# Inverting triangles of 16 on VectorE and joining them to 32 on TensorE, in a chunked linear-attention kernel with an MLP behind it

## The chip, the cores and the metric

The kernel runs on one core of one Trainium2 chip. The metric is the device time of one execution in microseconds; lower is better. The time of the kernel before is the median of three runs.

## The reference

For each of 4 x 8 = 32 heads, with 768 time steps and a head dimension of 40, a 40 x 40 state is carried from step to step:

```
y[t]  = r[t] @ state
Sa    = state @ a[t]
state = state * w[t] - outer(Sa, b[t]) + outer(v[t], k[t])
```

The outputs of all heads are laid side by side to rows of 320 numbers, 3072 rows in all, and go through an MLP: `h = x @ w_in` (320 to 2048), `g = h * tanh(softplus(h))`, `out = g @ w_out` (2048 to 320). All inputs and outputs are float32.

## The kernel before

**Chunks and heads.** The 768 steps are cut into 12 chunks of 64. Within a chunk the recurrence is written with matrices. For each chunk and head a 64 x 64 triangle of products between `a` and `b` has to be inverted; what is left of the recurrence is a few small products and a state that goes from chunk to chunk. The 32 heads are held as two halves `be` = 0 and 1, each with 16 heads.

**Units.** The program is written as units with short names, a letter, a chunk and a half or group:

- `l` loads `wa` (decays and `a`) and `bk` (`b` and `k`) of a chunk and a half by SyncE's queue. There are two buffers of each kind (`NWA = 2`), so that the load of a half waits until the half two places earlier is used up.
- `p` (scan, L287 to L302) forms running products of the decays on VectorE: a reduction L287, two scans L289 and L296, products L294 and L300.
- `g` (gram, L317) makes the products of `a` with `b` and `k` on TensorE. ScalarE copies them to `GP` (L318, L321), VectorE masks the other part to `HA` (L322).
- `k` (natural, L333, L339, L346) transposes `bk` and `a` on TensorE.
- `i` (inverse, L353 to L365) works on a pair of chunks, that is on 64 triangles of 64 x 64, each seen as two 32 x 32 triangles on its diagonal and one 32 x 32 square, the corner, below them. VectorE masks the 128 diagonal triangles, transposes them so that each lies along a partition, and inverts all at once by forward substitution: 30 steps, each a product L360 into `tmp` and a sum L362 into `XL`. Three transposes in all (L355, L364, L365) lay them in and out. A step needs the result of the step ahead of it.
- `b` (blocks, L390) and `m` (corner, L374 and L382) build the 64 x 64 inverse in `T64`: TensorE multiplies the square from the right and from the left by the two inverted triangles, ScalarE copies between (L378) and behind (L385). There are two tiles `T64`.
- `t` (merge, L401) multiplies `HA` by `T64`; `KT` is copied by ScalarE (L403).
- `V`, `A`, `B`, `T`, `D`, `C` are the steps of the state for a chunk and a group of heads: `A` L431, `T` L439, `D` L447, `B` L459 with VectorE's mask L462, `C` L481 and L488 with VectorE's L491 and L495.
- `v`, `u`, `q`, `o` are loads and stores by GpSimd's queue; `w` and `W` load the MLP's weights and split them in two parts on ScalarE and VectorE; `x` and `X` load the attention's result for the MLP; `h` (L653), `H` (L660, L661), `y` (L674 to L676) and `z` (L680) are the MLP.

**Order.** Two tables of names fix the order by hand. `SEQ` is the order in which the units are written down; `PLAN` gives for each engine how many instructions of which unit follow on one another. Each engine works its list strictly in that order. VectorE's list mixes the steps of an inverse with scans of later chunks, instruction by instruction. TensorE's list holds the MLP's first products (`h`) between the steps of the last two chunks, and nothing but the MLP after them.

**Buffers.** `g`, `k`, `t`, `m` and `h` write to one PSUM pool (`pa`) of two tiles, 4 KB per partition each. The inverse's `GP` has two tiles, `TT` and `XL` one.

A program's float32 product stands twice among the trace's matmuls: a row x64 in the trace is 32 products of the program. A product of fp32r (the MLP's) and a transpose stand once.

Of the kernel before, what the change touches and what calls it, by code (L numbers as in the profile page):

```python
# [2 lines left out]

# [5 lines left out]
F32 = mybir.dt.float32  # L9
# [10 lines left out]
NWA = 2  # L20
NKT = 4
NXL = 1
NTT = 1
NYEV = 1
# [198 lines left out]
def attention(ctx, tc, I, yD, pD, nch, M, U):  # L223
# [22 lines left out]
    with ln('z'):  # L246
# [5 lines left out]
        for t in T64[:NT64]:  # L252
            G.memset(t, 0.0)
# [12 lines left out]
    def ld(c, be):  # L266
# [8 lines left out]
        if (c, be) == (0, 0):  # L275
            LQ.dma_start(out=cst, in_=I['cst'])
# [519 lines left out]
```

## Time and profile before

| what | value |
|---|---|
| three runs | 750.04, 752.26, 752.87 us |
| median | 752.26 us |
| the profiled execution | 749.9 us, its span 748.1 us |
| TensorE's mean granted clock in it | 0.958 of full |
| busy share of the span: TensorE, VectorE, ScalarE, GpSimd | 87%, 61%, 48%, 14% |
| share of the chain that ended last: TensorE, VectorE, ScalarE, DMA | 68%, 15%, 6%, 5% |
| merges of the first pair of chunks begin, of the last pair | 96.1 us, 367.7 us |
| first product of the MLP begins | 392.6 us |

The profile is read in two stages. Up to some 390 us the attention runs, with many small products on TensorE and a full VectorE; behind that the MLP, with TensorE full. The span is shorter than the run's time by 1.8 us, which lie around it. The granted clock is that of TensorE alone: 1.00 is full speed. The profile's records of it begin at 101 us; what lies ahead of them is shown as full.

### The profile page before, as it was taken

To read this page: it belongs to the slowest core of one execution; us is meant where nothing else is said; L and a number is where in the kernel's file an instruction comes from. 1 tells how busy PE (TensorE), PEld (TensorE's weight loads), DVE (VectorE), ACT (ScalarE), POOL (GpSimd) and SP (SyncE) were. 2 spreads that over 40 slices of the span, in tenths; PEclk is the share of its full clock that TensorE was granted. 3 is DMA by queue.
4 is the path that set the end of the run, shared out by engine and by line. 5 is a ranking of instruction groups with operands and counts; after the bars stand their busy time and mean duration, and the time that the engine had idled before them with its cause. 6 is when DMAs were issued, how large, how long until landed. Compare 5 with 4: busy or idle time off the path is not lost.

```text
span 748.1 us, 22984 instructions
## 1 busy us (share of the span) xinstructions
PE 652.8 (87%) x10184; PEld 583.2 (78%) x10184; DVE 455.8 (61%) x901; ACT 359.2 (48%) x571; POOL 104.9 (14%) x181
## 2 busy tenths in 40 slices
PE   2645799789798879888889999999999999999997
PEld 1443688688687778777778889998988989989997
DVE  7689999799899999999267768521222122111100
ACT  2222556655575846687566655532333323323311
POOL 7211013223223313212120000000000000000000
PEclk9999999779879989979899999999999999999999
DMA  7433215334524624334266543130101100100001
GB/s 211 111 90 88 82 32 152 92 83 124 135 68 102 160 64 121 80 96 129 85 196 179 156 151 106 44 115 1 36 29 57 35 1 1 36 1 1 35 1 37
DMA packets 31348, 62.12 MB, mean 83 GB/s; under 512 B 6800, under 2 KB 19216, under 8 KB 31248
## 3 DMA queue, kind: packets, MB, share of 16 engines
q1 hardware_dynamic: 22800, 40.91, 18.3%
q0 software_dynamic: 8448, 19.73, 10.7%
q8 instruction: 80, 1.31, 0.8%
q14 instruction: 20, 0.16, 0.1%
HBM read 48.77 MB, written 11.80 MB: 81 GB/s over the span
## 4 chain that ended last, share of the span: by engine, by line
PE 68%; DVE 15%; ACT 6%; issue 6%; DMA 5%; SPq 0%; DVEq 0%; ACTq 0%
PE pa L653 24%; PE pu L676 4%; PE pu L674 4%; PE pu L675 4%; PE pq L676 4%; PE pq L675 4%; PE pq L674 4%; DMA wa<-in_wa 3%; PE pa L317 3%; PE pq L459 3%; DVE XL L362 3%; PE pq L481 3%; DVE tmp L360 3%; PE pa L401 2%; PE pa L333 2%
## 5 line engine op out<-in xcount | busy, mean ns | idle before, releaser
L661 DVE TENSOR_TENSOR gl<-g,gh 128x1024 fp32r<-128x1024 f32 x48 | 58.7, 1224 | 186.2 <-ACT gh L660 186.0
L653 PE MATMUL pa<-xh,w_ih 128*128 128x512 f32 x288 | 113.1, 393 | 0.0
L654 ACT ACTIVATE g<-pa 128x1024 f32<-128x1024 f32 x48 | 49.3, 1027 | 99.3 <-PE pa L653 86.1
L653 PE MATMUL pa<-xh,w_il 128*128 128x512 f32 x288 | 96.7, 390 | 0.0
L660 ACT CAST gh<-g 128x1024 fp32r<-128x1024 f32 x48 | 50.2, 1048 | 61.9 <-PE pq L675 58.7
L653 PE MATMUL pa<-xl,w_ih 128*128 128x512 f32 x192 | 74.8, 390 | 0.0
L317 PE MATMUL pa<-bk,wa 40*64 40x128 f32 x768 | 36.5, 337 | 35.5 <-DMA bk<-in_bk 14.2
L653 PEld LDWEIGHTS pa<-xh,w_il 128*128 128x128 f32 x288 | 54.1, 188 | 11.4
L653 PEld LDWEIGHTS pa<-xh,w_ih 128*128 128x128 f32 x288 | 54.1, 188 | 10.6
L362 DVE TENSOR_TENSOR XL<-XL,tmp 128x30 f32<-128x30 f32 (+9 forms) x180 | 59.0, 328 | 2.6
L360 DVE TENSOR_TENSOR tmp<-XL 128x30 f32<-128x30 f32 (+9 forms) x180 | 58.6, 326 | 2.8
L317 PEld LDWEIGHTS pa<-bk,wa 40*64 40x64 f32 x768 | 29.0, 169 | 39.8 <-DVE bk L300 25.9
L676 PE MATMUL pq<-w_oh,gl 128*128 128x320 f32 x192 | 59.3, 309 | 0.0
L676 PE MATMUL pu<-w_oh,gl 128*128 128x320 f32 x192 | 59.3, 309 | 0.0
L675 PE MATMUL pq<-w_ol,gh 128*128 128x320 f32 x192 | 59.3, 309 | 0.0
L674 PE MATMUL pq<-w_oh,gh 128*128 128x320 f32 x192 | 59.3, 309 | 0.0
L674 PE MATMUL pu<-w_oh,gh 128*128 128x320 f32 x192 | 59.2, 309 | 0.0
L675 PE MATMUL pu<-w_ol,gh 128*128 128x320 f32 x192 | 59.2, 308 | 0.0
L302 POOL DMA_DIRECT2D pD<-P x48 | 35.2, 738 | 127.7 <-DVE w L292 52.9
L481 PE MATMUL pq<-UVQ,bkn 128*64 128x104 f32 (+1 forms) x768 | 40.9, 262 | 11.7 <-DVE UVQ L462 7.1
L481 PEld LDWEIGHTS pq<-UVQ,bkn 128*64 128x64 f32 x768 | 36.4, 143 | 15.7 <-issue 9.1
L653 PEld LDWEIGHTS pa<-xl,w_ih 128*128 128x128 f32 x192 | 36.1, 188 | 6.2
(93 smaller groups left out, 1338.0 us busy)
## 6 DMA issues: line engine op xcount, KB each, us to landing
wa<-in_wa SPq DMA_DIRECT2D x48, 162.5 KB
bk<-in_bk SPq DMA_DIRECT2D x48, 160.0 KB
cv_d<-in_wi SPq DMA_DIRECT2D x12, 512.0 KB
cv_d<-in_wo SPq DMA_DIRECT2D x16, 320.0 KB
VS<-in_vN POOLq DMA_DIRECT2D x24, 160.0 KB, 4.1
bdr<-in_rD POOLq DMA_DIRECT2D x24, 160.0 KB, 3.6
pD<-P POOLq DMA_DIRECT2D x48, 80.0 KB, 3.0
UVT<-in_vD POOLq DMA_DIRECT2D x24, 160.0 KB, 3.9
```

The source lines that it names most:

```text
L302: PQ.dma_start(out=pD[c, be, :, al].rearrange("e (s t) -> e s t", t=64), in_=P3[al * 64:al * 64 + 40, :, 0:64])
L317: PE.matmul(pt[o, al, s // 2], a[q, s], bk[q, s], start=(s < 2), stop=True, skip_group_check=True)
L360: V.tensor_tensor(out=tv, in0=X[:, i + 1:32, i:i + 1].broadcast_to([128, 31 - i, i]), in1=X[:, i:i + 1, 0:i].broadcast_to([128, 31 - i, i] ...
L362: V.tensor_tensor(out=X[:, i + 1:32, 0:i], in0=X[:, i + 1:32, 0:i], in1=tv, op=ALU.add)
L481: PE.matmul(py[be * 64:be * 64 + 64, al, s, 0:n], BKN[c, be][:, u * 40:u * 40 + 64], UVQ[be][:, u, 0:n], start=(s == 0), stop=(c == 0), sk ...
L653: PE.matmul(pt[:, j], w, x, start=(n == 0), stop=(n == 7), skip_group_check=True)
L654: A.activation(g, pt, AF.Mish)
L660: A.copy(gh, g)
L661: V.tensor_tensor(out=gl, in0=g, in1=gh.bitcast(F32), op=ALU.subtract)
L674: PE.matmul(po[i][k], gh[:, j, t], oh, start=(f == 0), stop=False, skip_group_check=True)
L675: PE.matmul(po[i][k], gh[:, j, t], ol, start=False, stop=False, skip_group_check=True)
L676: PE.matmul(po[i][k], gl[:, j, t], oh, start=False, stop=(f == 15), skip_group_check=True)
```

## The change

**The inverse.** VectorE inverts triangles of 16 instead of 32. `inverse` transposes `GP` into `DD` (L367), masks the two 16 x 16 triangles on the diagonal of each 32 x 32 triangle into `XD` (L368), and does 14 steps of a product and a sum (L374, L376) on both triangles of a partition at once; two transposes (L378, L379) lay the result in `TT` and, transposed, in `DD`. The mask of 1024 numbers (L353) goes.

**The join.** A new unit `j` for each pair of chunks makes 32 x 32 inverses out of the 16 x 16 ones on TensorE, in four diagonal tiles of the array (partitions 0 to 31, 32 to 63, 64 to 95, 96 to 127, each with the same columns). It has one product with an identity in fp32r (L384), 128 small float32 products (L388), a copy by ScalarE to `Z` (L389), 128 products (L393), 64 products (L397), and five copies by ScalarE (L398, L401). All of them use one PSUM tile `pa`.

**The corner.** It is one unit for a pair of chunks instead of two, with the same 128 products (L413, L416), one copy between instead of two for each half, and four behind.

**Exchanged halves.** For the heads of `be` = 1 the two halves of a chunk in `a` are exchanged, so that their triangles come to lie on the other partitions of their tile; the copies of `gram` and `merge`, a mask and a scan's product (now two instructions) follow that.

**Loads and order.** Four buffers for `wa` and `bk` instead of two. `SEQ` and `PLAN` are new throughout.

```diff
-NWA = 2
+NWA = 4
+NDD = 1
 SEQ = '''
-    l0.0 l0.1 p0.0 p0.1 v0 g0.0 k0.0 u0 q0 g0.1 l1.0 k0.1 l1.1 p1.0 p1.1 g1.0 k1.0 g1.1 k1.1 l2.0 i0 l2.1 p2.0 p2.1 g2.0
+    l0.0 p0.0 l1.0 l1.1 l0.1 p0.1 p1.0 g0.0 k0.0 g0.1 p1.1 l2.0 p2.0 k0.1 g1.0 g1.1 i0 k1.1 l2.1 l3.1 g2.0 v0 u0 k1.0 l3.0
...
-    wa[..., 528:] = a.transpose(4, 2, 1, 6, 3, 0, 5).reshape(nch, 2, 2, 40, 512)
+    at = a.transpose(4, 2, 1, 6, 3, 0, 5).reshape(nch, 2, 2, 40, 8, 2, 32).copy()
+    at[:, 1] = at[:, 1, ..., ::-1, :].copy()
+    wa[..., 528:] = at.reshape(nch, 2, 2, 40, 512)
...
-        V.tensor_tensor(out=gp[:, :, 1], in0=gp[:, :, 1], in1=maskG.unsqueeze(1).broadcast_to([128, 32, 32]), op=ALU.mult)
-        X = iw.tile([128, 32, 32], F32, name="XL", bufs=NXL)
-        V.transpose(X.rearrange("p t j -> p j t"), gp[:, :, 1].rearrange("p u j -> p j u"))
-        V.memset(X.rearrange("p t j -> p (t j)")[:, 0:1024:33], 1.0)
-        for i in range(1, 31):
-            tmp = iw.tile([128, 240], F32, name="tmp", bufs=NTMP)
...
+        V.transpose(X0[:, 0:1024].rearrange("p (j t) -> p j t", t=32), gp[:, :, 1].rearrange("p u j -> p j u"))
+        V.tensor_tensor(out=d, in0=d0, in1=mask16.unsqueeze(1).broadcast_to([128, 2, 16, 16]), op=ALU.mult)
+        V.memset(XD[:, 0:1024:33], 1.0)
+        for i in range(1, 15):
+            m = 15 - i
+            tmp = iw.tile([128, 112], F32, name="tmp", bufs=NTMP)
+            tv = tmp[:, 0:2 * i * m].rearrange("p (b j t) -> p b j t", j=i, t=m)
+            V.tensor_tensor(out=tv, in0=d[:, :, i:i + 1, i + 1:16].broadcast_to([128, 2, i, m]),
+                            in1=d[:, :, 0:i, i:i + 1].broadcast_to([128, 2, i, m]), op=ALU.mult)
+            V.tensor_tensor(out=d[:, :, 0:i, i + 1:16], in0=d[:, :, 0:i, i + 1:16], in1=tv, op=ALU.add)
...
+    def join(n):
+        gp, tt, dd = GP[n], TT[n], DD[n]
+        pt = ps_a.tile([128, 2, 512], F32, name="pa").rearrange("p x (u t) -> p x u t", t=16)
+        PE.matmul(pt[:, 0], identR, eyeR.unsqueeze(1).broadcast_to([128, 32, 16]), start=True, stop=True, skip_group_check=True)
+        for u in range(32):
+            for k in range(4):
+                q = slice(k * 32, k * 32 + 32)
+                PE.matmul(pt[k * 32:k * 32 + 16, 0, u], gp[q, u, 1, 0:16], tt[q, u, 16:32], start=False, stop=True, skip_group_check=True)
+        A.copy(Z[:, :, 16:32], pt[:, 0])
+        for u in range(32):
+            for k in range(4):
+                q = slice(k * 32, k * 32 + 32)
+                PE.matmul(pt[q, 1, u], dd[q, u], Z[q, u, 16:32], start=(u == 0), stop=True, skip_group_check=True)
+        for c2, x in product(range(2), range(8)):
+            for h, be in product(range(2), range(2)):
+                q, u = slice(h * 64 + be * 32, h * 64 + be * 32 + 32), c2 * 16 + be * 8 + x
+                PE.matmul(pt[q, 0, u], Z[q, u], dd[q, u, 0:16], start=(c2 + x == 0), stop=True, skip_group_check=True)
+        A.copy(tt[:, :, 16:32], pt[:, 1])
+        for h, be in product(range(2), range(2)):
+            q = slice(h * 64 + be * 32, h * 64 + be * 32 + 32)
+            A.copy(pick(dd[q], be)[:, :, :, 0:16], pick(pt[q, 0], be))
...
-        A.copy(kt, pk)
+        k4, p4 = (x.rearrange("p h a s (y t) -> p (h a s) y t", y=2) for x in (kt, pk))
+        A.copy(k4[:, :, ::-1] if be else k4, p4)
```

**What moves, at three places.** The first is TensorE's list at the fifth pair of chunks, from the gram of chunk 11 to the merge of chunks 8 and 9. Before (L317 is `g`, L333, L339 and L346 are `k`, L447 is `D`, L374 and L382 are the corner, L401 is the merge):

```order
L317 MATMUL pa<-bk_93,wa_91 64x128 x16
L333 MATMUL pa<-cst,bk_93 128x128 x8
L447 MATMUL pu<-cst,ST_112 128x128 x4
L339 MATMUL pa<-cst,wa_91 128x128 x4
L374 MATMUL pa<-TT,GP 32x32 x32
L346 MATMUL pa<-w_4675,cst 64x16 x2
L346 MATMUL pa<-w_4868,cst 64x16 x2
L374 MATMUL pa<-TT,GP 32x32 x32
L382 MATMUL pa<-X_5208,GP 32x32 x32
L447 MATMUL pu<-cst,ST_113 128x128 x4
L382 MATMUL pa<-X_5278,GP 32x32 x32
L401 MATMUL pa<-T_95,HA 64x64
```

The same place now (L384, L388, L393 and L397 are the join, L413 and L416 the corner, L482 is `D`, L344 and L350 are `k`, L435 is the merge):

```order
L482 MATMUL pu<-cst,ST_125 128x128 x4
L384 MATMUL pa<-eyeR,identR 128x512
L388 MATMUL pa<-TT,GP 16x16 x128
L482 MATMUL pu<-cst,ST_126 128x128 x4
L393 MATMUL pa<-Z,DD 32x16 x128
L397 MATMUL pa<-DD,Z 32x16 x64
L413 MATMUL pa<-TT,GP 32x32 x64
L416 MATMUL pa<-X_6376,DD 32x32 x64
L344 MATMUL pa<-cst,bk_100 128x128 x8
L350 MATMUL pa<-cst,wa_96 128x128 x4
L435 MATMUL pa<-T_103,HA 64x64
```

The 128 products of the corner now have 321 of the join ahead of them, with one short step of the state (L482) between, and stand closed up instead of among other units.

The second place is VectorE's list where the first inverse begins. Before (L355 to L362 belong to the inverse, L287, L288, L289, L292 and L294 to a scan, L322 to a gram):

```order
L287 TENSOR_REDUCE w_474<-wa_90 128x8
L355 STREAM_TRANSPOSE XL<-GP 128x32x32
L288 RECIPROCAL d_94<-w_474 128x8
L356 MEMSET XL 128x32
L360 TENSOR_TENSOR tmp<-XL 128x30
L322 TENSOR_TENSOR HA<-pa,cst 128x8x64
L362 TENSOR_TENSOR XL<-XL,tmp 128x30
L289 SCALAR_TENSOR_TENSOR P<-wa_90,d_94 128x520
L360 TENSOR_TENSOR tmp<-XL 128x58
L292 COPY w_474<-P 128x8
```

Now (L307 ends a scan, L367 to L376 belong to the inverse):

```order
L307 SCALAR_TENSOR_TENSOR E<-wa_94,d_102 128x519
L367 STREAM_TRANSPOSE DD<-GP 128x1024
L368 TENSOR_TENSOR XD<-DD,cst 128x2x16x16
L369 MEMSET XD 128x32
L374 TENSOR_TENSOR tmp<-XD 128x28
L376 TENSOR_TENSOR XD<-XD,tmp 128x2x14
L374 TENSOR_TENSOR tmp<-XD 128x52
L376 TENSOR_TENSOR XD<-XD,tmp 128x2x2x13
L374 TENSOR_TENSOR tmp<-XD 128x72
```

The scan of chunk 2 that was mixed with the first steps of the inverse stands ahead of it now, and the first half of the steps follow on one another.

The third place is TensorE's list behind the grams of the first pair, now (L328 is `g`, L344, L350 and L357 are `k`, the other names are as above):

```order
L384 MATMUL pa<-eyeR,identR 128x512
L328 MATMUL pa<-bk_99,wa_95 64x128 x16
L388 MATMUL pa<-TT,GP 16x16 x64
L344 MATMUL pa<-cst,bk_99 128x128 x8
L388 MATMUL pa<-TT,GP 16x16 x64
L350 MATMUL pa<-cst,wa_95 128x128 x4
L393 MATMUL pa<-Z,DD 32x16 x64
L357 MATMUL pa<-w_275,cst 64x16 x2
L357 MATMUL pa<-w_834,cst 64x16 x2
L393 MATMUL pa<-Z,DD 32x16 x64
L328 MATMUL pa<-bk_100,wa_96 64x128 x16
L397 MATMUL pa<-DD,Z 32x16 x64
```

Here grams and transposes of chunks 2 and 3 stand between the join's parts; before, all of them stood ahead of the first corner.

More of the change, by code (lines that the diff above doesn't have):

```diff
@@ L2 @@
 from functools import partial
+from itertools import product
 import numpy as np
@@ L144 @@
+        h5.7 H5.7 z5.0 z5.1 z5.2 z5.3
     ''',
     'Pool': '''
[L146 to L149 removed]
@@ L213, in layouts @@
     p = np.arange(128)
-    cst = np.zeros((128, 288), np.float32)
+    cst = np.zeros((128, 608), np.float32)
     cst[:, :128] = np.eye(128)
@@ L293, in scan @@
         a3 = a.rearrange("p (s t) -> p s t", t=64)
-        V.scalar_tensor_tensor(out=a3, in0=a3, scalar=-1.0, in1=P3[:, :, 0:64], op0=ALU.mult, op1=ALU.mult)
+        for o, i in ((slice(0, 32), slice(32, 64)), (slice(32, 64), slice(0, 32))) if be else ((slice(0, 64), slice(0, 64)),):
+            V.scalar_tensor_tensor(out=a3[:, :, o], in0=a3[:, :, o], scalar=-1.0, in1=P3[:, :, i], op0=ALU.mult, op1=ALU.mult)
         V.reciprocal(d1[:, 64:584:65], w2[:, 1])
@@ L370, in corner, with pick @@
+    def pick(x, be):
+        return x.rearrange("p (c b s) t -> p c b s t", b=2, s=8)[:, :, be]
+    def corner(n):
+        gp, tt, dd = GP[n], TT[n], DD[n]
         pt = ps_a.tile([128, 2, 512], F32, name="pa").rearrange("p x (u t) -> p x u t", t=32)
-        for j in range(16):
-            for k in range(2):
-                q, o = slice(k * 64 + 32, k * 64 + 64), slice(k * 64, k * 64 + 32)
-                PE.matmul(pt[o, 0, j], gp[q, h * 16 + j, 0], tt[q, h * 16 + j], start=(j == 0), stop=True, skip_group_check=True)
@@ L375, in corner @@
         X = iw.tile([128, 16, 32], F32, name="X2", bufs=NX2)
-        for k in range(2):
-            q = slice(k * 64, k * 64 + 32)
-            A.copy(X[q], pt[q, 0])
-        for j in range(16):
-            for k in range(2):
-                q = slice(k * 64, k * 64 + 32)
-                PE.matmul(pt[q, 1, j], gp[q, h * 16 + j, 1], X[q, j], start=(j == 0), stop=True, skip_group_check=True)
-        for k in range(2):
-            q = slice(k * 64, k * 64 + 32)
-            A.copy(T64[n % 2][q, us, 32:64], pt[q, 1])
+        its = [(c2 * 8 + x, c2 * 16 + be * 8 + x, h * 64 + 32 - be * 32, h * 64 + be * 32)
+               for c2, x, h, be in product(range(2), range(8), range(2), range(2))]
@@ new lines, in corner @@
+        for j, u, q, o in its:
+            PE.matmul(pt[o:o + 32, 0, j], gp[q:q + 32, u, 0], tt[q:q + 32, u], start=(j == 0), stop=True, skip_group_check=True)
+        A.copy(X, pt[:, 0])
+        for j, u, q, o in its:
+            PE.matmul(pt[o:o + 32, 1, j], dd[o:o + 32, u], X[o:o + 32, j], start=(j == 0), stop=True, skip_group_check=True)
+        for h, be in product(range(2), range(2)):
+            q = slice(h * 64 + be * 32, h * 64 + be * 32 + 32)
+            A.copy(pick(T64[n % 2][q], be)[:, :, :, 32 - be * 32:64 - be * 32], pt[q, 1].rearrange("p (c s) t -> p c s t", c=2))
@@ L512, in attention @@
         U['i%d' % n] = partial(inverse, n)
+        U['j%d' % n] = partial(join, n)
         U['b%d' % n] = partial(blocks, n)
-        for h in range(2):
-            U['m%d.%d' % (n, h)] = partial(corner, n, h)
+        U['m%d' % n] = partial(corner, n)
     U['/p'] = pctx.close
```

240 lines of the change are left out of this document (121 added, 119 removed).

## The prediction

> **What bounds the kernel now.** I read the page first, then windows of the trace, then single stretches of its timeline. The page says which engine is full where:
>
> ```profile
> span 748.1 us, 22984 instructions
> PE   2645799789798879888889999999999999999997
> DVE  7689999799899999999267768521222122111100
> PEclk9999999779879989979899999999999999999999
> ```
>
> A digit is a slice of 18.7 us. VectorE is full from the second slice to the nineteenth. TensorE is full only from the twenty-second, where the MLP runs alone; ahead of that it has gaps, and its granted clock falls again and again. So there are two stages: an attention of some 390 us that VectorE seems to bound, and an MLP that TensorE bounds and that the change doesn't touch.
>
> The attention is periodic, with a period for each pair of chunks. The merges of the first and of the last pair, in the timeline of TensorE:
>
> ```profile
> 96.08 6.38 PE L401 MATMUL pa<-T,HA 64*64 64x64 f32 x256
> 367.66 1.92 PE L401 MATMUL pa<-T,HA 64*64 64x64 f32 x119
> ```
>
> Five periods take 367.7 - 96.1 = 271.6 us, 54.3 us each. Behind the last merge come 748.1 - 367.7 = 380.4 us. What the engines do within those five periods stands in one window (length, then busy time of TensorE, its weight loads, VectorE, ScalarE, GpSimd, then the clock):
>
> ```profile
> core 0: us, PE busy (x) PEld busy (x) DVE busy (x) ACT busy (x) POOL busy (x), PEclk, DMA share, GB/s
> 96.10:367.70 271.60, 232.27 (x6706) 207.35 (x6708) 244.47 (x565) 175.39 (x317) 70.00 (x122) 0.89 0.39 102
> ```
>
> For a period that is 48.9 us of VectorE (90%) and 46.5 us of TensorE (86%). TensorE has only 54.3 - 46.5 = 7.8 us of idle time in a period. That is the point on which all else turns: the change takes work from an engine that is 90% busy and gives work to one that is 86% busy.
>
> **What VectorE loses.** The inverse's steps and the mask, as groups of the whole execution (count, busy time, mean of one):
>
> ```profile
> L362 DVE TENSOR_TENSOR XL<-XL,tmp 128x30 f32<-128x30 f32 (+9 forms) x180 | 59.0, 328 | 2.6
> L360 DVE TENSOR_TENSOR tmp<-XL 128x30 f32<-128x30 f32 (+9 forms) x180 | 58.6, 326 | 2.8
> L353 DVE TENSOR_TENSOR GP<-GP,cst 128x1024 f32<-128x1024 f32 x6 | 7.3, 1225 | 10.1 <-ACT GP L321 10.0
> L322 DVE TENSOR_TENSOR HA<-pa,cst 128x512 f32<-128x512 f32 x24 | 16.4, 683 | 4.2 <-ACT GP L321 4.0
> L360 DVE TENSOR_TENSOR tmp<-XL 128x30 f32<-128x30 f32 x12 | 2.3, 190 | 0.2
> L362 DVE TENSOR_TENSOR XL<-XL,tmp 128x108 f32<-128x108 f32 x12 | 3.2, 268 | 0.2
> ```
>
> The 60 steps of an inverse cost (59.0 + 58.6) / 6 = 19.6 us. The 28 that replace them have 28 to 112 numbers for each partition, between the last two rows: 28 x 0.24 = 6.7 us (5.3 to 7.5). The new mask has 512 numbers, 0.68 us as L322 for 1.22 as L353. The three transposes stay. VectorE loses 13.4 us for each pair of chunks, about 80 us in all, and needs some 36 us in a period. The scan's product in two parts for half the heads, two more memsets and the queue of loads (four buffers: loads only come earlier) cost VectorE under 3 us in all. From then on VectorE doesn't set the period.
>
> **What TensorE gets.** A join has 320 float32 products of 32 rows and 16 moving columns, and one of 512 columns in fp32r. The nearest rows are the corner's products, 32 rows and 32 columns, at full and at half clock, and two others with full and half clock beside them (a float32 product is two matmuls of the trace):
>
> ```profile
> L374 PE MATMUL pa<-TT,GP 32*32 32x32 f32 x768 | 17.6, 207 | 8.8 <-issue 5.1 <-DVE TT L364 1.7 <-ACT rw L348 1.3
> 351.25 1.16 PE L374 MATMUL pa<-TT,GP 32*32 32x32 f32 x61
> 362.07 1.92 PE L382 MATMUL pa<-X,GP 32*32 32x32 f32 x64
> 349.14 1.16 PE L459 MATMUL pq<-bdr,UVT 40*64 40x64 f32 x64
> 118.40 1.10 PE L317 MATMUL pa<-bk,wa 40*64 40x128 f32 x32
> 259.30 2.08 PE L317 MATMUL pa<-bk,wa 40*64 40x128 f32 x32 [0.44 <-ACT T L385]
> ```
>
> The last matmul of a row lasts some 0.21 us by itself (the mean of L374), so the corner's matmuls follow at (1.16 - 0.21) / 60 = 16 ns at full clock and (1.92 - 0.21) / 63 = 27 ns at half. L459 has twice the columns of L374 and the same duration: fewer columns don't make such a product cheaper. So a product of the join takes 32 or 54 ns, and a join 321 x 0.032 = 10.3 us at full clock or 321 x 0.054 = 17.3 us at half. Which of the two is read from windows around a corner, 3.41 us each, with three rows of the timeline ahead of them:
>
> ```profile
> 253.75 1.70 PE L374 MATMUL pa<-TT,GP 32*32 32x32 f32 x95 [0.40 <-ACT bkn L334]
> 256.93 1.11 PE L382 MATMUL pa<-X,GP 32*32 32x32 f32 x59
> 273.40 2.08 PE L431 MATMUL pu<-KT,VS 104*64 104x64 f32 x64
> 254.83:258.24 3.41, 2.46 (x138) 2.31 (x132) 3.41 (x7) 3.09 (x7) 0.81 (x5) 1.00 0.66 187
> 258.24:261.66 3.42, 2.98 (x49) 2.25 (x49) 3.32 (x6) 3.32 (x7) 1.94 (x3) 0.50 0.57 141
> 261.66:265.07 3.41, 2.15 (x63) 2.01 (x58) 2.75 (x4) 2.24 (x5) 0.00 (x0) 0.50 0.03 8
> 265.07:268.48 3.41, 3.41 (x55) 3.02 (x57) 3.13 (x9) 1.12 (x2) 0.00 (x0) 0.50 0.08 12
> 268.48:271.89 3.41, 2.57 (x140) 2.27 (x132) 3.07 (x11) 1.64 (x3) 0.00 (x0) 1.00 0.56 177
> 271.89:275.30 3.41, 2.47 (x92) 2.38 (x91) 3.38 (x10) 2.07 (x3) 0.28 (x1) 1.00 0.04 14
> 275.30:278.72 3.42, 2.70 (x89) 2.27 (x87) 3.42 (x8) 1.06 (x3) 2.39 (x4) 1.00 0.49 114
> ```
>
> In the first of them TensorE is busy for 2.46 us, nearly all of it with the corner's small products; the window behind it is at half clock. In the window from 271.89 it is busy for 2.47 us with merges and a step of 104 rows, and the clock stays full. The same busy time, another outcome: what differs is how little of the array is at work. And the clock comes back only behind a window that larger products filled. A join uses the array less than a corner does and has two and a half times its products, so I take it at half clock: 17.3 us less about 0.2 us for the first of it, **17.1 us**.
>
> The Trainium skill says otherwise (TensorE: Matmul & The Clock Gate, Part 1: The HAM clock gate): the clock is halved after an idle window of about 3.4 us, and sustained work keeps it. By that page a join without gaps keeps full clock and takes the smaller of the two prices. The trace agrees with the length of the window (half-clock stretches begin and end on steps of 3.41 us), not with idleness as the cause (2.46 of 3.41 us busy).
>
> Work next to the join is slowed too: the two rows of L317 are one gram at full and at half clock, 1.10 and 2.08 us. Four to six such pieces (grams, transposes, steps) stand within a join or right behind the corner; the corner's own stretch of half clock paid for part of that before. I add **2 us** (0 to 5).
>
> ScalarE's copies, by the nearest rows:
>
> ```profile
> L378 ACT COPY X<-pa 32x512 f32<-32x512 f32 x24 | 13.8, 576 | 1.5 <-PE pa L382 1.3
> L321 ACT COPY GP<-pa 32x256 f32<-32x256 f32 x48 | 17.4, 363 | 0.9
> ```
>
> The old corner had eight copies of 512 numbers for a pair, 4.6 us; the join and the new corner have three of 512 and eight of 256, 3 x 0.58 + 8 x 0.36 = 4.6 us: no change, and ScalarE is busy for only 35 us in a period. What the join waits for, its copy to `Z`, has other matmuls behind it in most pairs; about 1 us stays in it.
>
> **What is absorbed.** TensorE no longer waits for VectorE. At best all 7.8 us of idle time go, and some of the busy time too: a run's tail of 0.2 us counts as busy, and it is hidden once the next run is ready. At worst the order of dependent steps keeps half of the idle time. I take **11 us** (4 to 14), as TensorE is then the engine that the others wait for.
>
> **The start.** The first inverse is what the first merge waits for:
>
> ```profile
> 2.01 4.83 DMA wa<-in_wa
> 42.12 2.10 DVE L355 STREAM_TRANSPOSE XL<-GP 128x1024 f32<-128x1024 f32 x1
> 84.61 1.91 DVE L364 STREAM_TRANSPOSE TT<-XL 128x1024 f32<-128x1024 f32 x1
> L300 DVE TENSOR_TENSOR bk<-bk,E 128x1024 f32<-128x1024 f32 x24 | 29.2, 1218 | 0.2
> L289 DVE TENSOR_TENSOR_SCAN P<-wa,d 128x520 f32<-128x520 f32 x24 | 29.6, 1233 | 0.1
> L296 DVE TENSOR_TENSOR_SCAN E<-wa,d 128x519 f32<-128x519 f32 x24 | 29.6, 1233 | 0.2
> L294 DVE SCALAR_TENSOR_TENSOR wa<-wa,P 128x512 f32<-128x512 f32 x24 | 16.4, 684 | 0.0
> ```
>
> It takes from 42 to 86 us now, since scans are mixed into it. A scan costs 1.22 + 1.23 + 1.23 + 0.68 and small rows, about 5.2 us. Now five scans and three masks stand ahead of the inverse, and the first load landed at 6.8 us, with a weight's load ahead of it that comes later now. So the inverse begins near 6 + 26 + 2 = 34 us. Until its last transpose VectorE has the 6.7 us of steps, 5 us of transposes and mask, a scan, most of another and three masks: some 22 us, to 56 us. But the join of 17 us, three grams and two chunks' halves of transposes at half clock (2.1 us and some 3 us each), and the corner of 256 x 0.027 = 6.9 us come behind it on TensorE; part of them overlaps the inverse. The first merge comes at about **90 us** (80 to 100), 6 us earlier than now. What the shorter inverse wins at the start, the join nearly takes back.
>
> **The sum.** A period: 54.3 + 17.1 + 2 - 11 = 62.4 us. Five of them behind 90 us: 402 us to the last pair's merge. Behind it as now 380.4 us, since no inverse follows. The span: 782.4 us; with the 1.8 us around it 784 us. The profiled execution's 749.9 us lie 2.4 us under the median of the three runs, so on the median's scale the forecast is **786 us**. TensorE becomes the bound of the attention too.
>
> **The rivals.** *The clock holds.* If a join that runs without gaps doesn't lose the clock more often than the corner does now, it costs 10.3 us, and the neighbours nothing: 54.3 + 10.3 - 11 = 53.6 us, the time 90 + 268 + 380.4 + 1.8 + 2.4 = 743 us. For it: the join is dense. Against it: the windows above.
>
> *The four diagonal tiles run together*, the rival that ends faster. The corner alternates between two diagonal tiles and takes 32 ns a product; with four tiles and 16 columns up to four products could share that time. A join then takes 3 to 9 us; with 5 us and 8 us absorbed (there is less need to) a period is 51.3 us and the time 90 + 257 + 380.4 + 4.2 = 731 us. It decides from about 35 ns a product down: there the join equals what is absorbed. Against it: L459 uses four tiles (two ranges of rows, two of columns) and isn't faster than L374 with two.
>
> The Trainium skill lets different tiles load weights and multiply in parallel (TensorEngine Tiling, Key Properties); by that the join would be this cheap. No run here shows four diagonal tiles.
>
> *The join starves its neighbours*, a worse outcome: it holds one of two `pa` tiles for all of its time, so grams, transposes and merges in it must each wait for their copy. With 8 waits of about 1 us a period is 70 us and the time 825 us.
>
> **How the numbers follow.** A measurement of this kernel can tell half a per cent, 4 us, from no change. Half clock with the sum above has 0.64; its own range comes from its bounds: the period between 56 and 68 us, since not all ends fall together, and the start, give 752 to 812 us. The clock holds: 0.10. Four tiles: 0.10. Starved: 0.12. Others: 0.04. The range from 742 to 815 us takes in the first rival and leaves out the second and most of the third. Faster: 0.19 (four tiles, most of a held clock). The same: 0.07. Slower: 0.74.
>
> **What would show it.** Right: VectorE's busy time falls by about 80 us and its slices up to 370 us show gaps; the join's matmuls (L388, L393, L397) follow at 25 to 30 ns, PEclk shows 0.5 in stretches of 20 us or more for each pair; first merge near 90 us, merges 62 us apart; TensorE's idle time in the attention is nearly gone. Wrong: join matmuls under 16 ns, a clock as before, merges 54 us apart or fewer, or idle time on TensorE that stays.

## The result, and the profile after

The kernel after takes 818.57 us (median of four runs, 817.10 to 819.34); the kernel before took 752.57 us beside it (four runs). The ratio is 1.087, 95% interval 1.0821 to 1.0919: slower by 8 to 9%. The forecast was 786 us with a range from 742 to 815. The sign was right; what follows shows that the mechanism behind it wasn't. The ratios below leave out runs over 1.5% longer than the fastest of their kernel, which concerns e4 and e8 alone.

The page of the profiled execution after:

```profile
span 816.5 us, 30503 instructions
PE   3477879796969588958887899999999999999997
DVE  8898934792658057815622786673122322102110
PEclk9565959795679689966669999999999999999999
q8 instruction: 110, 1.80, 0.9%
PE 78%; issue 10%; DVE 5%; ACT 4%; SPq 1%; DMA 1%; DVEq 0%; ACTq 0%
```

A slice is 20.4 us. VectorE has the gaps that the forecast named, and PEclk its dips; but TensorE, which the forecast had filled, has gaps too up to the twenty-third slice. In the last line, the chain of work that ended last, "issue" has 10% where it had 6%: time in which TensorE waited for nothing that the profile shows. The fifth line had no part in the forecast. It is a DMA queue of kind "instruction", with packets and megabytes. Before it read:

```profile
q8 instruction: 80, 1.31, 0.8%
```

1.80 MB in 110 packets are 16,384 bytes each (1,802,240 bytes in all).

From the first pair's merge on, the same window as in the prediction (length, then busy time of TensorE, its weight loads, VectorE, ScalarE, GpSimd), with the first merge's row from the timeline:

```profile
85.70:433.60 347.90, 276.14 (x9872) 245.48 (x9871) 189.13 (x399) 175.66 (x325) 68.25 (x120) 0.78 0.30 82
```

```profile
85.70 2.09 PE L435 MATMUL pa<-T,HA 64*64 64x64 f32 x128
```

The first merge comes at 85.7 us (forecast 90), the last pair's at 433.6, so a period is 347.9 / 5 = **69.6 us** (forecast 62.4; before 54.3). Behind it stand 816.5 - 433.6 = 382.9 us (forecast 380.4). The span misses the forecast's 782.4 us by 34.1 us, and 35.9 us of that lie in the five periods. VectorE is busy for 54% of them instead of 90%, and yet they are longer.

The join itself, as groups (count, busy time, mean of one, then TensorE's idle time ahead of them):

```profile
L393 PE MATMUL pa<-Z,DD 32*32 32x16 f32 x1536 | 22.4, 202 | 12.4 <-issue 12.3
L388 PE MATMUL pa<-TT,GP 32*16 32x16 f32 x1536 | 15.5, 180 | 19.5 <-issue 19.1 <-DVE TT L378 0.4
L397 PE MATMUL pa<-DD,Z 32*32 32x16 f32 x768 | 12.8, 209 | 7.7 <-issue 7.7
```

Nearly 40 us of idle time stand ahead of the join's matmuls, nearly all of it "issue". The timeline shows where:

```profile
180.86 0.37 PE L388 MATMUL pa<-TT,GP 32*16 32x16 f32 x31
182.48 1.21 PE L388 MATMUL pa<-TT,GP 32*16 32x16 f32 x128 [1.25 <-issue]
188.68 0.99 PE L388 MATMUL pa<-TT,GP 32*16 32x16 f32 x97 [4.99 <-issue]
189.60 1.12 PE L494 MATMUL pq<-bdr,UVT 40*64 40x64 f32 x30
192.52 1.22 PE L494 MATMUL pq<-bdr,UVT 40*64 40x64 f32 x34 [1.79 <-issue]
```

Two things are to be seen. 128 matmuls take 1.21 us: taking off the last one's 0.18 us, (1.21 - 0.18) / 127 = **8.1 ns** each, not 27. And the stalls come at a fixed count: 128 matmuls between the first two, 97 + 30 = 127 to the third (a record is missing now and then). 128 matmuls with their 128 weight loads are 256 instructions, and 16,384 / 256 = 64 bytes each. So a stall falls where a packet of queue q8 ends. The totals fit too: the 14,030 matmuls and as many weight loads of the trace fill 109.6 such packets, those of before (10,184 of each) 79.6. Over the whole trace, 42 of the 44 distances between neighbouring stalls of more than 0.3 us lie within 6 of a multiple of 128 matmuls. The DMA queues in the two windows from 186.25 to 187.30 us and from 189.7 to 191.1 us each show one packet:

```profile
q8 instruction: 1, 0.02, 5.5%
```

```profile
q8 instruction: 1, 0.02, 5.7%
```

They land at 187.23 and 191.07 us by their records, and the stalls end at 188.68 and 192.52, 1.45 us behind each. Of 33 such stalls over 0.7 us, 31 end between 1.1 and 1.9 us behind the landing of a packet. The shortest distances between the starts of two packets lie close together: in the five periods none is under 3.35 us, and a quarter of them are under 3.6. 3.5 us for 128 matmuls are 27 ns for one. That is the price that the forecast had put on the array at half clock.

Some packets come later than that. Five stalls of 3.06 to 5.57 us make up 22.8 us of the issue time in the five periods. While each of their packets was awaited, from the start of the packet before, the other queues kept the DMA engines busy for 54 to 79% of the time. Two lines of the window from 182.5 to 186.25 us, in which the stall of 4.99 us begins:

```profile
q1 hardware_dynamic: 158, 0.53, 44.2%
q0 software_dynamic: 159, 0.44, 39.2%
```

Whether these loads and stores delayed the packet isn't shown; other stalls beside as much traffic were short.

The Trainium skill (Runtime: NRT & Kernel Launch, Instruction fetch mechanics) describes such blocks of 16 KiB or 256 instructions, which the trace bears out, and calls the cost of crossing one "mostly hidden". Here it isn't: in the five periods 57.8 us of TensorE's idle time are issue, against 11.6 us before.

### The profile page after: what moved, and what is told of

Its sections match the earlier page's. It is cut to its first block, busy times and chain, and to the rows that moved or that the text cites. A ratio compares the mean times of both kernels' runs of the same rounds, so it can differ in the third digit from the quotient of the medians.

```text
span 816.5 us, 30503 instructions
## 1 busy us (share of the span) xinstructions
PE 699.0 (86%) x14030; PEld 624.5 (76%) x14030; DVE 397.9 (49%) x723; ACT 364.5 (45%) x592; POOL 107.3 (13%) x184
## 4 chain that ended last, share of the span: by engine, by line
PE 78%; issue 10%; DVE 5%; ACT 4%; SPq 1%; DMA 1%; DVEq 0%; ACTq 0%
PE pa L688 22%; PE pq L516 5%; PE pq L494 4%; PE pu L710 3%; PE pu L711 3%; PE pu L709 3%; PE pq L711 3%; PE pq L709 3%; PE pq L710 3%; PE pu L466 3%; PE pa L328 3%; PE pa L435 3%; PE pu L474 3%; PE pa L393 3%; PE pa L344 3%
## 5 line engine op out<-in xcount | busy, mean ns | idle before, releaser
L696 DVE TENSOR_TENSOR gl<-g,gh 128x1024 fp32r<-128x1024 f32 x48 | 58.6, 1223 | 187.4 <-ACT gh L695 187.4
L695 ACT CAST gh<-g 128x1024 fp32r<-128x1024 f32 x48 | 50.0, 1048 | 57.9 <-PE pq L710 56.0
L497 DVE TENSOR_TENSOR UVQ<-pq,cst 128x512 f32<-128x512 f32 x48 | 31.0, 684 | 65.5 <-PE pq L494 65.5
L328 PE MATMUL pa<-bk,wa 40*64 40x128 f32 x768 | 37.2, 338 | 17.3 <-DMA cst<-in_cst 13.1
L516 PE MATMUL pq<-UVQ,bkn 128*64 128x104 f32 (+1 forms) x768 | 46.0, 279 | 2.6 <-DVE UVQ L497 1.2
L516 PEld LDWEIGHTS pq<-UVQ,bkn 128*64 128x64 f32 x768 | 40.6, 155 | 6.8 <-issue 3.6
L328 PEld LDWEIGHTS pa<-bk,wa 40*64 40x64 f32 x768 | 29.7, 170 | 20.1 <-DVE bk L311 13.1
L494 PE MATMUL pq<-bdr,UVT 40*64 40x64 f32 x1536 | 34.1, 239 | 7.2 <-issue 5.5
```

Source lines behind the costliest of these rows:

```text
L328: PE.matmul(pt[o, al, s // 2], a[q, s], bk[q, s], start=(s < 2), stop=True, skip_group_check=True)
L494: PE.matmul(pq[x:x + 64, al, be, s], UVT[q, g * 4 + s, be * 128 + x:be * 128 + x + 64], br[q, be, g * 4 + s], start=(be == 0 and s == 0), ...
L497: V.tensor_tensor(out=UVQ[be][:, g * 8:g * 8 + 8, 0:64].rearrange("p (s a) t -> p a s t", a=2), in0=pq[:, :, be], in1=maskQ.unsqueeze(1).u ...
L516: PE.matmul(py[be * 64:be * 64 + 64, al, s, 0:n], BKN[c, be][:, u * 40:u * 40 + 64], UVQ[be][:, u, 0:n], start=(s == 0), stop=(c == 0), sk ...
L695: A.copy(gh, g)
L696: V.tensor_tensor(out=gl, in0=g, in1=gh.bitcast(F32), op=ALU.subtract)
```

## The experiments

The theories: SUPPLY, that TensorE runs out of instructions; ARRAY, that the join costs what its products take in the array, with the half clock that they bring; ORDER, that the new lists and the held tile do it. The ratios are to the kernel before, run beside each on the same chip. A profile's period is from the first to the last pair's first merge, a fifth of it.

| kernel | first merge | period | behind the last | ratio (95%) |
|---|---|---|---|---|
| before | 96.1 | 54.3 | 380.4 | 1 |
| after | 85.7 | 69.6 | 382.9 | 1.087 (1.082 to 1.092) |
| e1 join hollow | 82.3 | 53.0 | 384.6 | 0.982 (0.976 to 0.989) |
| e2 join, one tile after another | 100.8 | 78.1 | 383.7 | 1.175 (1.169 to 1.182) |
| e3 join with 1 column | 85.9 | 68.3 | 383.3 | 1.088 (1.081 to 1.095) |
| e4 half the products, twice as wide | 81.7 | 58.6 | 385.4 | 1.012 (1.000 to 1.023) |
| e5 before + join | 110.7 | 71.0 | 381.9 | 1.136 (1.131 to 1.141) |
| e6 after + wide products | 87.9 | 69.0 | 381.8 | 1.097 (1.090 to 1.104) |
| e7 after, joined column tiles | 86.6 | 74.1 | 386.1 | 1.133 (1.128 to 1.138) |
| e8 before, joined column tiles | 95.6 | 61.1 | 385.5 | 1.055 (one run) |
| e9 before without steps | 92.8 | 51.8 | 380.0 | 0.984 (0.978 to 0.990) |
| e10 after without steps | 82.0 | 67.8 | 385.1 | 1.084 (1.078 to 1.090) |
| e11 before + join's products in the MLP | 95.4 | 53.0 | 428.1 | 1.062 (1.056 to 1.068) |

The attention of e11 is that of before, unchanged: 53.0 and 54.3 us show how far a period differs from one execution to another. e1 to e4, e5 to e8 and e9 to e11 ran on three chips, where the kernel before took 744.51, 747.13 and 745.27 us. e4's period is that of its profiled execution, 761.64 us, where its four runs took 750.19 to 762.84 us.

**e1: the join without its small products.**

```diff
         PE.matmul(pt[:, 0], identR, eyeR.unsqueeze(1).broadcast_to([128, 32, 16]), ...)
+        PE.matmul(pt[:, 1], identR, eyeR.unsqueeze(1).broadcast_to([128, 32, 16]), ...)
-        (the three loops of L385 to L397)
```

> Leaves out the join's 320 small products for each pair (its two wide products, its copies, the held tile and the whole order stay; the output is not the reference's). Three theories. SUPPLY: TensorE's instructions come in packets of 16,384 bytes (queue q8 of the DMA: 80 packets before, 110 after), never less than 3.5 us apart, and the dense small products run out of them; without the join 30 packets go, some 30 x 3.5 = 105 us of supply, until another engine sets the time: 700 to 745 us, q8 back to 80, TensorE's idle time put down to issue from 69 us to under 30. ARRAY (the products' own time and the half clock that they cause): the join's busy time goes, 54 us and some of the slowed neighbours: 740 to 765 us, the issue gaps unchanged in kind. ORDER (the held tile, the waits and the place of the work): little changes, over 800 us.

Measured: 733.37 us. The window of its five periods:

```profile
82.30:347.20 264.90, 220.26 (x6677) 194.04 (x6676) 188.87 (x399) 173.91 (x325) 68.18 (x120) 0.90 0.38 106
```

So the join's products, with what they do to their neighbours, cost 69.6 - 53.0 = **16.6 us** a period, some 80 us in all; the copies and the order cost little: ORDER falls. q8 shows 80 packets again, and the idle time put down to issue falls from 69.2 to 22.3 us in the whole execution, as SUPPLY expected. The time alone doesn't tell SUPPLY from ARRAY: 0.982 of the 752.57 us is 739 us, 1 us from ARRAY's range. But the row says something more. Of the join only two wide products and the copies are left, VectorE has nearly a quarter less to do than before (188.87 us for 244.47), and the period is 53.0 us, hardly less than before.

**e2: the tiles one after another.**

```diff
-        for u in range(32):
-            for k in range(4):
-                q = slice(k * 32, k * 32 + 32)
+        for k in range(4):
+            q = slice(k * 32, k * 32 + 32)
+            for u in range(32):
```

(and so for the second and the third loop)

> The join's loops swapped, tile outside and matrix inside, so that 32 (or 16) products in a row use the same diagonal tile instead of four in turn. The same instructions, the same output. SUPPLY: the rate is set by the packets, not by the array: 810 to 828 us, even though the matmuls of a burst follow more slowly. ARRAY: a matmul goes from 8 ns to the corner's 16 to 27 ns, 640 x 6 of them, 30 to 70 us more: 850 to 890 us. ORDER: no change.

Measured: 876.59 us, as ARRAY expected and against SUPPLY. Its groups and one row of its timeline:

```profile
L393 PE MATMUL pa<-Z,DD 32*32 32x16 f32 x1536 | 78.4, 207 | 0.0
L388 PE MATMUL pa<-TT,GP 32*16 32x16 f32 x1536 | 40.8, 178 | 4.5 <-issue 3.8 <-DVE TT L378 0.7
L397 PE MATMUL pa<-DD,Z 32*32 32x16 f32 x768 | 38.7, 210 | 0.0
```

```profile
206.81 3.31 PE L388 MATMUL pa<-TT,GP 32*16 32x16 f32 x128 [0.42 <-issue]
217.85 6.82 PE L393 MATMUL pa<-Z,DD 32*32 32x16 f32 x128
```

The stalls are nearly gone (11.2 us of issue in the five periods, about as in the kernel before), for the array is now the slower one: (3.31 - 0.18) / 127 = 25 ns for a matmul of L388 on one tile, and (6.82 - 0.21) / 127 = 52 ns for one of L393, which has 32 weight columns instead of 16 and lies in a stretch of half clock there. In the kernel after the same two follow at 8 and, at half clock, 13.6 ns. So both limits are real, and the larger holds: the packets' 27 ns, or the array's. The expectation's mistake was to take the packets as the only one. The Trainium skill (TensorEngine Tiling, Key Properties) lets different tiles load and multiply in parallel; 25 against 8 ns agrees with it.

**e3: one moving column.** The same instructions, with a sixteenth of the work.

```diff
-PE.matmul(pt[k * 32:k * 32 + 16, 0, u], gp[q, u, 1, 0:16], tt[q, u, 16:32], ...)
+PE.matmul(pt[k * 32:k * 32 + 16, 0, u, 0:1], gp[q, u, 1, 0:16], tt[q, u, 16:17], ...)
```

(and so for the second and the third loop, with one more wide product for the rest of the tile)

> The join's 320 products with 1 moving column instead of 16: the same number of instructions with a sixteenth of the columns (and one wide product more for the rest of the tile; the output is not the reference's). SUPPLY: no change, 805 to 825 us, q8 110 packets. ARRAY: most of what the hollow join gains, under 780 us. ORDER: no change.

Measured: 813.28 us, the same ratio as the kernel after (1.088 and 1.087).

```profile
L394 PE MATMUL pa<-Z,DD 32*32 32x1 f32 x1536 | 23.5, 186 | 11.1 <-issue 11.1
L389 PE MATMUL pa<-TT,GP 32*16 32x1 f32 x1536 | 15.0, 164 | 16.2 <-issue 16.1
```

The same time, nearly the same busy time and stalls (50.7 us of issue in the five periods for 57.8). SUPPLY holds, and ARRAY, which expected under 780 us, falls.

**e4: half as many products, each twice as wide.**

```diff
-        for u in range(32):
+        for u in range(0, 32, 2):
-                PE.matmul(pt[q, 1, u], dd[q, u], Z[q, u, 16:32], ...)
+                PE.matmul(pt[q, 1, u:u + 2], dd[q, u], Z[q, u:u + 2, 16:32], ...)
```

(and so for the other two loops)

> Half as many products in the join with twice the moving columns each (160 products of 32 columns; the same columns in all, half the instructions; every second matrix is left out as weights, so the output is not the reference's). SUPPLY: 15 packets fewer, 15 x 3.5 = 53 us: 757 to 780 us, q8 at 95. ARRAY: the same columns pass: 805 us or more. ORDER: no change, over 805 us.

Measured: 761.04 us, ratio 1.012.

```profile
q8 instruction: 95, 1.56, 0.8%
```

The same columns in half the instructions take back 7.5 of the 10.5 points between the hollow join and the kernel after (6.5 to 8 from the longest to the shortest of e4's runs). It is more than half; that the first packets still fit into slack would explain it, but no run shows it.

**e5: the old kernel with the join's products added.**

```diff
+    def join(n):
+        tt = TT[n]
+        pt = ps_a.tile([128, 2, 512], F32, name="pa").rearrange("p x (u t) -> p x u t", t=16)
+        for u in range(32):
+            for k in range(4):
+                q = slice(k * 32, k * 32 + 32)
+                PE.matmul(pt[k * 32:k * 32 + 16, 0, u], tt[q, u, 0:16], tt[q, u, 16:32], ...)
...
+'j0*320' (to 'j5*320') ahead of the first 'm' of each pair in PLAN
```

> The kernel before, with 320 products of the join's sizes added for each pair, four diagonal tiles in turn, in one piece ahead of the corner (nobody reads them; VectorE keeps its 60 steps). SUPPLY: 30 packets of instructions more, 110 on q8; the hollow join put the price of those 30 at some 80 us in the new order; the old one has more slack, so 40 to 80 us more: 790 to 830 us, and stalls put down to issue within the burst. ORDER (the new order and VectorE's changed list are what makes the join dear): at the measured 8.2 ns for a matmul a burst is 640 x 8.2 ns = 5.3 us, within TensorE's idle time of a period: under 775 us.

Measured: 848.51 us, above the range of SUPPLY and far from ORDER's. One burst of it:

```profile
156.45 1.90 PE L378 MATMUL pa<-TT 32*32 32x16 f32 x128 [1.75 <-issue]
160.18 1.90 PE L378 MATMUL pa<-TT 32*32 32x16 f32 x128 [1.82 <-issue]
```

```profile
110.70:465.70 355.00, 279.28 (x9904) 251.25 (x9904) 234.10 (x539) 174.64 (x317) 68.32 (x120) 0.79 0.29 79
```

128 matmuls, a stall, 128 matmuls, a stall, 3.73 us from one start to the next. A period is 71.0 us: the join costs 71.0 - 54.3 = 16.7 us with the old inverse, order and buffers too, and nothing of it fits into TensorE's idle time. The first merge comes 14.6 us later as well; in the new order, with other work between the join's parts, the products cost 3.4 us there (85.7 us for 82.3 in e1).

**e6: wide products among the small ones.**

```diff
+                if k == 3 and u % 16 == 15 and u < 32:
+                    for _ in range(3):
+                        PE.matmul(pt[:, 1], identR, eyeR.unsqueeze(1).broadcast_to([128, 32, 16]), ...)
```

(in the first loop; in the second loop the same into `pt[:, 0]`)

> The kernel after with 12 wide products (128 rows, 128 weights, 512 columns, 0.43 us each at full clock) put into each join, three behind each of its first four pieces of 64, into a half of the tile that is not in use. SUPPLY: a wide product is one instruction pair, and while it runs the next packet comes; the 31 us of array work fill stalls: 805 to 825 us, the issue gaps shorter, and if the clock holds up, somewhat less time. CLOCK (the half clock, 145 us of it behind the first merge, is what costs): the array is kept busy, the clock holds, the time falls under 790 us. ARRAY (the join's array time is added): 72 x 0.43 us more, 840 us or more.

Measured: 817.47 us, ratio 1.097, about 1% above the kernel after; the intervals just overlap.

```profile
87.90:432.70 344.80, 292.60 (x9930) 253.04 (x9929) 188.39 (x397) 175.38 (x325) 68.24 (x120) 0.82 0.30 83
```

The five periods, 69.0 us each, hold 60 of the 72 wide products, which are busy for 24.8 us there, and are no longer than without them: TensorE's busy time is 16 us longer, and issue has 38 us instead of 58. So most of the wide products lie in the stalls, as SUPPLY expected. The half clock falls from 150 to 123 us, and CLOCK's 790 us are not reached. What the regained clock saved by itself isn't told apart from what the wide products cost.

**e7 and e8: fewer instructions, by joining column tiles.**

```diff
-                    for x in (slice(0, 64), slice(64, 104)):
-                        PE.matmul(pk[x, h, al, s], ha[q, al, s, x], T64[...], ...)
+                    PE.matmul(pk[:, h, al, s], ha[q, al, s], T64[...], ...)
...
-                    for x in range(0, 128, 64):
-                        PE.matmul(pq[x:x + 64, al, be, s], UVT[q, g * 4 + s, be * 128 + x:be * 128 + x + 64], ...)
+                    PE.matmul(pq[:, al, be, s], UVT[q, g * 4 + s, be * 128:be * 128 + 128], ...)
```

> The kernel after with the merge's and step B's products for two column tiles put into one product of 104 or 128 weight columns: half as many instructions in those two (L435 and L494: 1,536 matmuls fewer, 12 packets), the same numbers. SUPPLY: 12 packets x 2.6 to 3.5 us less: 770 to 790 us, q8 at 98. ARRAY: two column tiles worked side by side before, so nothing is saved in the array: 810 us or more.

> The same joining of products in the kernel before, a version that computes the same. SUPPLY: q8 at 68; VectorE is the bound there, and only part of the 22.7 us of issue gaps can go: 5 to 25 us less, 725 to 745 us where the kernel before takes 750. ARRAY or VectorE alone: no change within half a per cent, or slower where the single products take longer.

Measured: 845.47 us for e7. e8's four runs took 788.19 to 809.53 us; the shortest, which is the profiled one, is 1.055 times the median of before beside it. Both are slower, and SUPPLY's expectations fail, for the reason of e2. The instructions did go: q8 shows 98 and 68 packets, as expected, and the issue in the five periods falls from 57.8 to 40.4 us in e7 and from 11.6 to 2.1 in e8. But TensorE's busy time in them rises by 45 us in e7 (276.1 to 321.1) and by 51 us in e8 (232.3 to 283.6). The first merges of e8's first and last pair, beside those of before in the prediction (256 matmuls in 6.38 us, 119 in 1.92):

```profile
95.57 11.36 PE L400 MATMUL pa<-T,HA 64*104 64x64 f32 x128
400.92 3.15 PE L400 MATMUL pa<-T,HA 64*104 64x64 f32 x64
```

By the starts of their records, a joined matmul follows at 86 ns in the first pair and a half of it at 24 ns; the clock isn't on record there. In the last pair, at full clock in both, it is 46 ns for a joined one and 14.6 ns for a half. Either way two halves take less time than one joined product. Fewer instructions help only where the products still take turns on different tiles.

**e9 and e10: VectorE's steps left out.**

```diff
-        for i in range(1, 31):
-            ...
         TT[n] = iw.tile([128, 32, 32], F32, name="TT", bufs=NTT)
```

(e9; in e10 the loop of L370 to L376, `range(1, 15)`)

> The kernel before without the 60 steps of each inverse on VectorE (19.6 us a pair by its rows; the mask, the clearing and the three transposes stay, and the last two transposes keep their place in VectorE's list; the inverse is not computed, so the output is not the reference's). It asks whether VectorE, 90% busy, set the period before. BOUND (the prediction's reading): the period falls from 54.3 us towards TensorE's 46.5 us of busy time, 5 x 7 us, and the first merge comes some 15 us earlier: under 705 us. WAITS (TensorE waited for VectorE in only 9.1 of the 271.6 us of five periods, by what ended its idle time): the period falls by no more than 2 us, and what is gained is the start: 715 to 740 us.

> The kernel after without the 28 steps of each inverse on VectorE (transposes, mask and clearing stay, at their places; the output is not the reference's). SUPPLY: VectorE no longer matters in the periods: they stay at 69.6 us within 1.5, the start is up to 7 us earlier: 800 to 818 us. BOUND: if the inverse is still on the path of each pair, 6.7 us go in every period: under 785 us.

Measured: 734.23 us (0.984) and 808.40 us (1.084). The window of e9:

```profile
92.80:351.60 258.80, 228.02 (x6706) 203.50 (x6704) 168.33 (x271) 174.96 (x317) 69.78 (x122) 0.90 0.40 107
```

VectorE has 33.7 us of work a period instead of 48.9, and the period is 51.8 us instead of 54.3: VectorE did not set it. TensorE's waits for VectorE in the five periods of before had said so:

```profile
PE pq L481 <- DVE UVQ L462: 7.1, 7, 2.2
PE pq L459 <- DVE UVQ L462: 1.1, 1, 1.1
PE pu L447 <- DVE stn L491: 0.9, 1, 0.9
```

Those are all of them: 9.1 us in 271.6, 1.8 us a period. WAITS holds, though the period fell by a little more than its 2 us; against e11, whose attention is that of before on the same chip (53.0 us), it fell by 1.2 us. In e10 the period falls by 1.8 us, a little more than SUPPLY allowed; as a time it isn't told apart from the kernel after.

**e11: the same products where supply is not short.**

```diff
+            for u in range(12 if q < 7 else 0):
+                for k in range(4):
+                    r = slice(k * 32, k * 32 + 32)
+                    PE.matmul(pb[i][3][r, 320 + u * 16:336 + u * 16], gh[r, 0, 0:32].bitcast(F32), gh[r, 1, 0:16].bitcast(F32), ...)
```

> The kernel before with 2,016 small float32 products of the join's sizes (32 rows, 32 weight columns, 16 moving columns, four diagonal tiles in turn; a join has 320, six joins 1,920) in the MLP, 48 of them behind the wide products of each unit of its second layer but the last of a block, written to columns that nobody reads. There the wide products take 0.3 us and more for one pair of instructions. SUPPLY: 31 packets more, but 46 of them in 380 us are never short, so that only the array's time is added, 4,032 x 8.2 ns = 33 us: 770 to 795 us. PRODUCT (a small product costs some 50 ns wherever it stands, by its weight load, its start or the half clock that it brings): 100 us as in the burst ahead of the corner, 840 us or more.

Measured: 793.43 us. The group of the added products:

```profile
L681 PE MATMUL pq<-gh 32*32 32x16 f32 x4032 | 41.7, 180 | 0.0
```

No idle time ahead of them, and 48 us for 4,032 matmuls: 12 ns each, of which 8.6 ns is the array's rate within a burst. About as many packets more (31 here, 30 there) cost 101 us in e5. So a small product isn't dear by itself; it is dear among others like it, and most products of the attention are small. PRODUCT falls.

## Why the prediction was right in sign and wrong in size

- **The price of the join** (17.1 us, and 2 us for its neighbours): measured 16.6 and 16.7 us in two orders. The number was nearly right by luck, for its working was wrong. The forecast read 27 ns a matmul off a corner at half clock; the join's matmuls follow at 8 ns, and what makes 640 of them cost 17 us is five packets of instructions, 5 x 3.5 = 17.5 us. Its own sign of being wrong, "join matmuls under 16 ns ... or idle time on TensorE that stays", came true on both counts (8 ns; TensorE's idle time in the five periods rose from 39.3 to 71.8 us). One reading behind it was unsound: L459 differs from L374 in its size and in its tiles at once, so that their equal time shows nothing about either alone. e3 shows that fewer moving columns aren't cheaper, and e2 that four tiles in turn are.
- **What is absorbed** (11 us, 4 to 14) is the step that failed. It rested on an attention "that VectorE seems to bound", read from its 90% busy time. Measured: 1.3 us (e1) to 2.5 us (e9), and a period differs by 1.3 us from one execution to another. The wait rows above, 1.8 us a period, were in the trace of before; the forecast took all of TensorE's idle time for a wait for VectorE. In the kernel after, TensorE's waits for VectorE are 1.8 us in the five periods instead of 9.1, so 1.5 us a period went. With the 16.7 us of e5 for the join and these 1.5 us in the place of the 11, the sum is 54.3 + 16.7 - 1.5 = 69.5 us a period; measured 69.6.
- **VectorE's 13.4 us a pair, 80 us in all.** The steps' rows fell as forecast, to (20.1 + 19.9) / 6 = 6.7 us an inverse (the two rows below). But the busy time fell by 57.9 us only (455.8 to 397.9). The durations of all VectorE's instructions fell by 77.6 us (501.5 to 423.9). But records of neighbouring instructions overlap, by 45.7 us in all before and 26.0 us after, so a sum of rows is more than the time that goes.
- **The corner**, which the forecast left as it was, got cheaper in the array. Its products now take turns on four tiles instead of two, and their busy time fell from 17.6 + 21.6 = 39.2 us in all to 9.9 + 11.7 = 21.6 us (the four corner rows below). What that is worth in time isn't shown: 10.2 us of issue stand ahead of L416 in the five periods.
- **The start** (90 us, 80 to 100) and **the end** (380.4 us) held: 85.7 and 382.9 us.
- **The rivals.** "Four diagonal tiles run together" had the array right (8 ns, under its 35 ns) and the time wrong, since the next limit stood right behind. "The clock holds" fell: 150 us of the five periods are at half clock, 61 us before. "The join starves its neighbours" gave 825 us, near the result, by another mechanism than the one at work: TensorE's waits for ScalarE's copies in the five periods fell from 18.1 us before to 11.3 us after.
- **Not settled.** What holds the period at 52 to 53 us when either VectorE's steps or the join are gone: TensorE is busy for 83 to 88% of it, and its waits are small ones for ScalarE's copies and for issue. Nor what keeps the packets 3.5 us apart, when one takes some 1 us. No version that computes the same and beats the kernel before came out of this: e1, in which the join's small products are left out, is 1.8% faster (0.976 to 0.989 of before), and that is about the most that this change could have given in this order.

```profile
L376 DVE TENSOR_TENSOR XD<-XD,tmp 128x28 f32<-128x28 f32 (+6 forms) x84 | 20.1, 239 | 2.2
L374 DVE TENSOR_TENSOR tmp<-XD 128x28 f32<-128x28 f32 (+6 forms) x84 | 19.9, 237 | 2.3
```

The corner before (L374, L382) and after (L413, L416), on TensorE:

```profile
L374 PE MATMUL pa<-TT,GP 32*32 32x32 f32 x768 | 17.6, 207 | 8.8 <-issue 5.1 <-DVE TT L364 1.7 <-ACT rw L348 1.3
L382 PE MATMUL pa<-X,GP 32*32 32x32 f32 x768 | 21.6, 229 | 3.6 <-ACT X L378 3.6
L413 PE MATMUL pa<-TT,GP 32*32 32x32 f32 x768 | 9.9, 209 | 4.1 <-issue 2.8 <-ACT TT L398 1.4
L416 PE MATMUL pa<-X,DD 32*32 32x32 f32 x768 | 11.7, 219 | 12.5 <-issue 10.8 <-ACT X L414 1.5
```

## What to carry to other kernels

Before work is moved off a busy engine, look at who waits for it: the waits of the engine that sets the end, by what ended them, are worth more than a busy share of 90%. Count the instructions too: where small products stand close together, divide the spacing of the instruction packets by the 128 matmuls (with their weight loads) that one holds, and take the larger of that price and the array's. A burst that stalls under "issue" every 128 matmuls is the sign of it; fewer and wider products help, as long as neighbours still use different tiles.

## What the runs showed of the hardware that was not expected

- TensorE's instructions came in packets of 16,384 bytes, which never started less than 3.25 us apart in any of the thirteen traces; a stall ended about 1.4 us behind the landing of one (1.1 to 1.9 us in 31 of 33).
- A float32 matmul of 32 rows, 16 weight columns and 16 moving columns followed at 8 ns with four diagonal tiles in turn and at 25 to 26 ns on one tile, at full and at half clock alike. With 32 weight columns it was 8.5 ns at full and 13.6 ns at half clock in four tiles, 49 to 52 ns at half clock on one. With 1 moving column instead of 16 (e3) four tiles gave the same figures. The corner's products, 32 weight and 32 moving columns, followed at 16 ns at full and 27 ns at half clock on two tiles in turn before, and at 8.6 and 13.6 ns on four after.
- The clock falls without idleness: in the five periods of e2 TensorE was busy for 364.09 of 390.50 us, and the mean granted clock was 0.73. In two windows of 3.41 us that follow on one another (the last two rows below), the first of them filled with L388's products on one tile after another, it fell from 1.00 to 0.50, and TensorE was busy throughout both by its records.

```profile
100.80:491.30 390.50, 364.09 (x9870) 336.67 (x9869) 189.17 (x400) 175.59 (x325) 68.24 (x120) 0.73 0.26 73
293.79:297.20 3.41, 3.41 (x149) 3.41 (x146) 0.00 (x0) 0.00 (x0) 0.61 (x1) 1.00 0.79 207
297.20:300.61 3.41, 3.41 (x132) 3.37 (x132) 0.00 (x0) 0.57 (x1) 0.00 (x0) 0.50 0.17 55
```
